# A new order for a clustered attention with a SoLU layer: the first batch's pairs one after another, its first marks copied by three engines

## The chip, the cores and the metric

One core of a Trainium2 chip. The metric is the device time of one execution in microseconds (us). Engines are named as in the profile: PE (TensorE matmul; PEld its weight loads), DVE (VectorE), ACT (ScalarE), POOL (GpSimd), SP (SyncE, which issues nearly all DMAs here).

## The reference

Four batches, eight heads, 768 tokens, 64 channels. Every query and key of a head goes to one of 16 clusters (the largest normalised product with the head's centroids); a query sees the keys of its own cluster only. The 3072 tokens, all heads side by side (512 channels), then pass a layer with 1024 hidden channels.

```python
q_assign = np.argmax(np.einsum('bhsd,hcd->bhsc', q_n, c_n), axis=-1)
k_assign = np.argmax(np.einsum('bhsd,hcd->bhsc', k_n, c_n), axis=-1)
mask = q_assign[:, :, :, None] == k_assign[:, :, None, :]
scores = np.where(mask, scale * np.matmul(q, k.transpose(0, 1, 3, 2)), -1000000000.0)
attn = softmax(scores)                       # over the keys
x = np.matmul(attn, v)  ->  [3072, 512]
...
h = x @ w_in
solu = h * softmax(h)
ln = (solu - mean(solu)) / np.sqrt(var(solu) + 1e-06) * g_ln
return ln @ w_out
```

## The kernel before, in words

**Steps and lists.** All work is recorded as small named steps (a kind and an index), each with an engine. `Weave.ORDER` (lines 28 to 73) is a list for each engine, written by hand as kinds with counts: "S2 V3" means the next two S steps, then the next three V steps. `AWAY` (74 to 90) names the steps that go to another engine than their default. Each engine works through its list in that order. Which S or V is next follows from `UNITS`, `GROUPS` and `BANKS` (256 to 313), the order in which the heads and query blocks are taken.

**Attention.** The unit of heads is a pair (two heads, 128 channels); four pairs a batch, sixteen in all.

- `ld`, `lv` (SP): loads of q, k and of v. Batch 0 is loaded with tokens on the partitions and turned on PE (`tp`, line 382; copied back to SBUF by `xa`, 389), the other batches are turned in blocks of 32 by DVE (`xt`, 404).
- `ca` (423): cast of q or k of one head to bf16 into the tile `qk`; `cv` (531): cast of v.
- `cl` (438, PE): scores of tokens and centroids; `tb`, `mx`, `oh`, `ot` (456 to 494, DVE): turned back, maximum, one-hot marks, turned again; `pl` (498): the marks are copied under the channels of `qk`, four copies a pair (or a half pair), so that one matmul over 80 or 96 rows gives score and mask together; `bl` (521): the other head's marks blanked.
- `S` (594, PE): one bank of scores, 512 columns in most units: two key tiles by 256 queries. Three score banks (`sps`). `E` (604, ACT): the exponential of a bank, 294 in all. Nine tiles (`e`).
- `V` (615, PE): the sum over the values for 128 queries of one head, six matmuls, 192 in all. `N` (628, DVE): normalisation of a group of up to six V into `x`. There is one tile `ops` for the groups' sums, so a group's first V waits for the N of the group before (line 1055).

Pair (0, 0) is done in two halves, so that the first scores can start on half of the tokens. In batch 0 before, the other three pairs were taken by thirds of the queries: `FIRST` (line 280) gives the first and second thirds of pairs 1, 2, 3 in turn, then the last thirds. The other batches take, for pairs 0 to 2, all queries of one head and then all of the other; pair 3 by thirds; the last batch ends by query tiles.

**Second half.** 24 token tiles of 128. `tx` (677, DMA transpose by SP, two tiles at a time; the last by PE, `ptx`): x turned, once all heads of those tokens are normalised. `h` (708, PE): four steps of two matmuls into `hreg`, three banks. `hm` (714, DVE): the maximum; `ex` (719, ACT): the exponential of 1024; `u` (725, DVE): the product; `tu` (730, DMA transpose by SP; last two tiles by PE, `ptu`); `bn`, `ag` (735, 740, DVE): statistics; `at`, `al` (745, 751, POOL): the factor alpha; `y` (760, PE): four steps of two matmuls; `sc` (776, ACT or DVE): scaled by alpha; `ou` (793, SP): stored.

**Weights.** w_in is loaded (`li`) and cast (`wi`); w_out is loaded (`lo`), scaled by g and centred, so that the layer's mean need not be taken off: `gt`, `gk`, `gs` turn and spread g, `su` (570, PE) sums w_out's rows, `sk` (578) copies the sums to SBUF, `me` (583, PE) spreads their mean, `ce` (586, DVE) writes the centred rows. `wm` and `fl` are matmuls on nothing, at the start (line 854).

`run` (124) works out a time for each step from the steps' costs; it sets the order in which steps are recorded, and no step's place in its engine's list.

Of the kernel before, what the change touches and what calls it, by code (L numbers as in the profile page):

```python
# [22 lines left out]
class Weave:  # L23
# [5 lines left out]
    ORDER["SP"] = """
        ld4 lv si ld4 lv lg ld4 lv2 ld4 lo2 ld4 lo ld3 lo ld3 li4 tx ld3 lv3 tx ld4 tu ld9 lv ld tu  # L30
        tx ld3 tu ld3 ou ld2 ou ld tu ld12 tu ld4 lv ld2 ou tx ld3 tu ou ld2 tx lv ld tu ld4 tx ld
        tu ou2 ld lv ld4 tu ld4 tu ld ou ld7 pl ou ld lv2 ld3 tu lv tx ou tu lv pl ld4 ou2 tx lv tu
        tx ou tu pl2 tu2 tx tu tx ou2 tx ou tu tx2 ou tu2 ou2 tu2 ou6
    """
    ORDER["POOL"] = """
        po z ca2 pl2 cv z bl pl2 ca z ca pl2 ca z2 ca3 cv ca cv ca pl3 sg ca cv2 pl3 ca2 gs pl ca cv
        ca wi ca pl2 wi3 bl ca pl2 cv at cv pl ca pl al bl at cv ca pl ca pl cv ca3 al at ca al ca
        at ca pl2 bl cv pl2 ca4 at ca2 al ca pl2 bl pl2 cv2 ca3 al at pl2 bl pl2 ca pl al ca3 at cv
        at pl ca pl2 ca2 pl al cv2 bl cv2 pl2 ca pl al pl at al at pl2 ca3 at al bl cv pl2 bl cv2
        ca3 pl5 al cv3 at al ca2 cv ca cv ca2 at ca2 pl ca al pl2 at2 pl3 at ca cv al at2 al2 at2 al  # L40
        at al3 at al2 at2 al2
    """
    ORDER["PE"] = """
        wm tp2 cp tp cl tp fl5 cl fl4 S3 tp2 S2 tp S cq S tp S2 tp2 S2 V3 S cl S tp2 V3 S gt S tp S
        tp S2 cl S2 V2 S V S2 tp S2 tp S2 V2 S V S2 cl S2 V2 S V2 S3 V S2 V2 S2 V S cl S3 su S2 V3 S
        V S3 V3 S2 V S su S2 V S V3 S3 me S3 V4 S3 cl S3 V4 S2 h S h S2 h S h S2 V3 S2 V h S h V S V
        S h S V S V S h S2 V3 S2 V h S2 h V2 S y3 S2 h3 S3 y V3 h V S2 V2 S cl S3 h2 S2 V3 S y2 S V
        h2 S V y2 S h S V h S2 h S y3 S2 y V3 h S3 cl V2 S V S y S2 y2 S3 V3 S y S2 V3 S2 cl S V S2
        V2 S h S2 V2 S V S h S2 V2 cl V2 S3 y2 S V S2 V y S2 y V2 S3 h2 S V h S h S2 V h S V S V y2
        S h V y2 S2 V S h3 S cl V S2 V2 S h V cl S3 h2 V y V S3 y2 V S h V3 S y S h S2 h2 S3 V2 y h  # L50
        S V S2 y V3 y S3 h3 y S3 V3 S h S V S V cl S V S h S cl V2 S3 y V2 S y S2 y V2 S3 h y V S3 V
        h V2 S3 cl S2 V2 S y3 S2 y S V3 S V S y S2 V S V3 S2 y2 S3 y V2 S2 h V2 S3 h3 S V S2 V y S V
        h2 V2 S y S2 y V y S h2 S3 cl h V S2 V3 S h V2 S3 h2 S y S2 V h S2 V y2 V4 S3 y h S2 h V h V
        S V S y2 S3 V3 h2 S2 h2 S2 y2 S V S h2 S V3 S2 h S h S2 V S y V2 S V y2 S2 h2 S2 h2 V2 S2 V2
        y S2 h V2 h V S2 h S V h S3 V2 h y S V y3 V h3 S2 y3 S2 y h2 V2 h y h y3 h V h V y4 h ptx h
        y4 h2 y3 h2 y ptu2 y6 ptu2 y6
    """
    ORDER["DVE"] = """
        cn cb xa ca tb mx oh ot pl2 tb mx oh ot xa3 bl cf cv xa zo xa2 tb ca mx oh gk N ot tb pl mx
        xa2 oh xa cv N ot tb pl N xt mx xt N oh ot tb pl2 ca N pl xt mx N sk oh N ot xt ce3 N tb ce5  # L60
        N hm mx N u oh ot bn N bn ag hm xt2 u N bn2 hm ag sc xt u N bn tb hm mx bn oh ag u xt bn ot
        xt N cv hm bn ag sc xt tb mx N u xt oh ot sc N bn2 xt ag xt tb N hm mx tb N oh ot u xt mx N
        bn oh bn xt hm ot ag N cv u bn2 xt hm tb mx u N tb oh mx hm ot bn2 oh ag u N sc ag hm bn ot
        u bn N xt2 ag xt2 hm tb N bl mx tb bn2 oh u N xt ag xt sc hm ot tb mx oh N bn sc N u bn N ag
        xt ot bn ca N mx sc oh hm u bn ag N xt hm bn2 bl tb u ot ag N hm mx bn2 u bn N oh ot hm bl2
        u ag N cv hm sc bn u N hm ag bn N bn u bn2 hm ag2 N bn u bn2 N ag hm bn u N ag hm bn2 u bn2
        hm sc u N ag2 bn tx hm bn sc u bn ag hm bn tu ag u bn2 tu ag sc
# [1182 lines left out]
```

## Time and profile before

| | us |
|---|---|
| median of 3 runs | 225.69 (225.38 to 227.81) |
| the profiled execution | 225.95 |
| its span, first to last instruction | 223.9 |

The span is what the profile shows; about 2 us of the execution lie around it. A row of the list of instruction groups reads: line, engine, operation, what it writes and reads, count, then busy time, mean ns of one, and the engine's idle time before it. Some of the costliest:

```
L607 ACT ACTIVATE e<-sps 128x512 bf16<-128x512 f32 (+1 forms) x294 | 151.0, 599 | 12.2 <-PE sps L601 10.2
L727 DVE TENSOR_TENSOR u<-e_sb,hreg 128x1024 bf16<-128x1024 bf16 x24 | 29.0, 1210 | 4.9 <-ACT e_sb L722 4.7
L738 DVE BATCH_NORM_STATS2 bs<-u 128x6 f32<-128x512 bf16 x48 | 31.5, 676 | 0.2
L716 DVE TENSOR_REDUCE nmax<-hreg 128x1 f32<-128x1024 f32 x24 | 29.0, 1209 | 2.6 <-PE hreg L710 2.2
L722 ACT ACTIVATE e_sb<-hreg,nmax 128x1024 bf16<-128x1024 f32 x24 | 26.9, 1120 | 4.5 <-DVE nmax L716 4.4
```

The first score begins at 10.16 us, the first attention exponential at 10.52, the first tile's exponential `ex` at 50.4, the last one at 214.6; the last matmul ends at 220.7.

### The profile page before, as it was taken

To read this page: it belongs to the slowest core of one execution; us is meant where nothing else is said; L and a number is where in the kernel's file an instruction comes from. 1 tells how busy PE (TensorE), PEld (TensorE's weight loads), DVE (VectorE), ACT (ScalarE), POOL (GpSimd) and SP (SyncE) were. 2 spreads that over 40 slices of the span, in tenths; PEclk is the share of its full clock that TensorE was granted. 3 is DMA by queue.
4 is the path that set the end of the run, shared out by engine and by line. 5 is a ranking of instruction groups with operands and counts; after the bars stand their busy time and mean duration, and the time that the engine had idled before them with its cause. 6 is when DMAs were issued, how large, how long until landed. Compare 5 with 4: busy or idle time off the path is not lost.

```text
span 223.9 us, 6574 instructions
## 1 busy us (share of the span) xinstructions
PE 215.1 (96%) x2388; PEld 148.1 (66%) x2420; DVE 197.3 (88%) x359; ACT 191.5 (86%) x371; POOL 127.1 (57%) x247
## 2 busy tenths in 40 slices
PE   7899999999999999999999999999999999999993
PEld 3576756677667678776677667777677687754442
DVE  3799899899999989999998989887998889888981
ACT  3689999999998999998889899999999998982362
POOL 3489843964794999547668634943895413031331
PEclk9999999999999999999999999999999999999999
DMA  7998989999898989999999999199931433766622
GB/s 152 353 318 147 249 199 275 290 243 158 132 199 140 232 130 165 193 189 177 183 218 168 184 195 195 65 174 232 236 64 28 79 70 120 96 146 170 176 97 94
DMA packets 125679, 38.80 MB, mean 173 GB/s; under 512 B 115016, under 2 KB 121168, under 8 KB 125648
## 3 DMA queue, kind: packets, MB, share of 16 engines
q1 hardware_dynamic: 123904, 37.87, 80.6%
q10 hardware_dynamic: 1744, 0.52, 1.0%
q8 instruction: 19, 0.31, 0.6%
q14 instruction: 12, 0.10, 0.2%
HBM read 23.11 MB, written 6.29 MB: 131 GB/s over the span
## 4 chain that ended last, share of the span: by engine, by line
PE 86%; ACT 5%; DVE 3%; issue 3%; DMA 1%; POOL 1%; ACTq 0%; DVEq 0%; POOLq 0%
PE sps L601 28%; PE hreg L710 18%; PE yps L771 16%; PE ops L624 14%; ACT e L607 5%; PE csc L450 4%; PE hreg L386 2%; PE hreg L574 1%; PE hreg L771 1%; DMA c_all<-in_centroids_dram 1%; PE csc L445 1%; DVE bs L738 1%; DVE u L727 1%; ACT xt L393 0%; PE hreg L584 0%
## 5 line engine op out<-in xcount | busy, mean ns | idle before, releaser
L607 ACT ACTIVATE e<-sps 128x512 bf16<-128x512 f32 (+1 forms) x294 | 151.0, 599 | 12.2 <-PE sps L601 10.2
L601 PE MATMUL sps<-qk 80*128 80x256 bf16 (+5 forms) x636 | 93.8, 264 | 1.8 <-POOL qk L514 0.7
L601 PEld LDWEIGHTS <-qk 80*128 80x128 bf16 (+1 forms) x636 | 60.2, 121 | 27.9 <-issue 9.0
L624 PEld LDWEIGHTS <-e 128*128 128x128 bf16 x1152 | 50.4, 97 | 12.3 <-issue 1.9
L624 PE MATMUL ops<-v,e 128*128 128x65 bf16 x1152 | 55.0, 193 | 0.1
L710 PE MATMUL hreg<-w_in_sb,xT 128*128 128x512 bf16 x173 | 49.1, 379 | 1.1
L771 PE MATMUL yps<-w_out_c,uT 128*128 128x512 bf16 x171 | 46.4, 379 | 0.6
L727 DVE TENSOR_TENSOR u<-e_sb,hreg 128x1024 bf16<-128x1024 bf16 x24 | 29.0, 1210 | 4.9 <-ACT e_sb L722 4.7
L514 POOL COPY qk<-oht 32x384 f32<-32x384 f32 (+1 forms) x50 | 24.4, 488 | 15.8 <-DVE oht L494 13.6
L738 DVE BATCH_NORM_STATS2 bs<-u 128x6 f32<-128x512 bf16 x48 | 31.5, 676 | 0.2
L716 DVE TENSOR_REDUCE nmax<-hreg 128x1 f32<-128x1024 f32 x24 | 29.0, 1209 | 2.6 <-PE hreg L710 2.2
L722 ACT ACTIVATE e_sb<-hreg,nmax 128x1024 bf16<-128x1024 f32 x24 | 26.9, 1120 | 4.5 <-DVE nmax L716 4.4
L433 POOL CAST qk<-xt 64x768 bf16<-64x768 f32 (+1 forms) x31 | 26.1, 842 | 5.5 <-DVE xt L393 3.9
L771 PEld LDWEIGHTS <-uT 128*128 128x128 bf16 x200 | 18.2, 97 | 12.3 <-DVE uT L704 0.7
L754 POOL TENSOR_SCALAR esq<-es,mv 128x1 f32<-128x1 f32 x24 | 8.5, 355 | 29.0 <-DVE mv L742 20.8
L435 POOL TENSOR_SCALAR qk<-xt 64x768 bf16<-64x768 f32 (+1 forms) x28 | 23.0, 820 | 1.7
L710 PEld LDWEIGHTS <-xT 128*128 128x128 bf16 x192 | 16.8, 97 | 9.4 <-issue 0.6
L407 DVE STREAM_TRANSPOSE xt<-raw 128x768 f32<-128x768 f32 x24 | 22.6, 953 | 0.2 <-DMA raw<-in_q_dram 0.2
L748 POOL TENSOR_SCALAR es<-esum 128x1 f32<-128x1 f32 x24 | 5.3, 221 | 27.6 <-ACT e_sb L722 27.1
L649 DVE TENSOR_TENSOR x<-ops,den 128x256 bf16<-128x256 f32 (+1 forms) x39 | 18.9, 486 | 1.3
L757 POOL TENSOR_TENSOR alpha<-esq,halves 128x1 f32<-128x1 f32 x24 | 13.5, 561 | 2.0
L786 ACT ACTIVATE y<-yps,alpha 128x512 f32<-128x512 f32 x13 | 9.0, 692 | 6.4 <-PE yps L771 6.0
(80 smaller groups left out, 170.1 us busy)
## 6 DMA issues: line engine op xcount, KB each, us to landing
vf<-in_v_dram SPq DMA_DIRECT2D x16, 384.0 KB, 4.4
out_dram<-y SPq DMA_DIRECT2D x23, 256.0 KB, 2.7
raw<-in_q_dram SPq DMA_DIRECT2D x50, 96.0 KB, 3.7
raw<-in_k_dram SPq DMA_DIRECT2D x50, 96.0 KB, 3.0
w_g<-in_moe_w_out_dram SPq DMA_DIRECT2D x4, 512.0 KB, 5.3
w_st<-in_moe_w_in_dram SPq DMA_DIRECT2D x4, 512.0 KB, 5.9
raw<-in_q_dram SPq DMA_DIRECT2D x3, 384.0 KB, 6.3
raw<-in_k_dram SPq DMA_DIRECT2D x3, 384.0 KB, 6.8
```

Of the source, the lines that this page charges most:

```text
L433: VEC[e].tensor_copy(dst, src)
L435: VEC[e].tensor_scalar(dst, src, scalar1=inv_C, scalar2=1.0, op0=Alu.mult, op1=Alu.mult)
L514: ins = VEC[e].tensor_copy(dst.bitcast(F32), src.bitcast(F32).unsqueeze(1) .to_broadcast([NB, 2, n // 2]))
L601: nc.tensor.matmul(sps_[n, k][:, c0:c0 + w], side(b, h // 2, 1, h % 2, keys)[r], side(b, h // 2, 0, h % 2, slice(s0 * P, s0 * P + w))[r])
L607: nc.scalar.activation(es[n, k][:, :w], sps_[n, k][:, :w], Act.Exp, scale=exp_scale, bias=-exp_scale)
L624: nc.tensor.matmul(opss[g][:, s, :VW], es[n, k][:, c0:c0 + P], v1[slot(b, h // 2)][:, h % 2, kt, :VW], start=(kt == 0), stop=(kt == n_t - 1))
L710: uses(nc.tensor.matmul(hreg[:, at(f, f2)[1], :], xTs[f][:, dc, :], w_in_sb[:, dc, f2 * FF2:(f2 + 1) * FF2], start=(dc == 0), stop=(dc == ...
L716: uses(nc.vector.tensor_reduce(ff[f, "nmax"][:], pair_of(f), axis=AXY, op=Alu.max, negate=True), *both(f))
L722: uses(nc.scalar.activation(ff[f, "e"][:], pair_of(f), Act.Exp, bias=ff[f, "nmax"][:], accum_out=ff[f, "esum"][:]), *both(f))
L727: uses(nc.vector.tensor_tensor(ff[f, "u"][:], ff[f, "e"][:], pair_of(f), op=Alu.mult), *both(f))
L738: nc.vector.bn_stats(ff[f, "bs"][:, f2, :], ff[f, "u"][:, f2, :])
L771: ins = nc.tensor.matmul(dst, ff[f, "uT"][:, at(f, f2)[0] * (n_fc // 2) + c, :], w_out_c[:, fc, cols], start=(fc == 0), stop=(fc == n_fc - 1))
```

## The change

Batch 0 loses its own order: pairs 1 and 2 are now taken as in the other batches, all queries of a head in one go (groups of six V), pair 3 by thirds. The marks of a step in halves may be copied by ACT too. The other edits outside the lists are numbers for `run` (`wm` 3.55 to 3.9, `tp`).

```diff
-    FIRST = [(p, s) for p in range(1, n_pair) for s in range(2)] + [(p, 2) for p in range(1, n_pair)]
     for b in range(B):
...
-            elif b == 0:
-                if p == 1:
-                    for p2, s in FIRST:
-                        GROUPS.append([unit(b, "A", 2 * p2 + j, s) for j in range(2)])
-                        for n in GROUPS[-1]:
-                            in_order(n)
             elif b < B - 1 and p < n_pair - 1 or b == B - 1 and p < n_first:
...
         elif e == "SP":
             ins = nc.sync.dma_start(out=dst, in_=src.unsqueeze(1).to_broadcast([NB, 2, n]))
+        elif e == "ACT":
+            ins = nc.scalar.copy(dst, src.unsqueeze(1).to_broadcast([NB, 2, n]))
...
-                costs = ({"DVE": 0.3, "POOL": 0.41} if half else
+                costs = ({"DVE": 0.3, "POOL": 0.41, "ACT": 0.42} if half else
```

All five lists and `AWAY` are written anew. The ACT list and what goes to ACT and DVE:

```diff
     ORDER["ACT"] = """
-        wa xa2 ca2 xa ca2 E12 xa2 E6 xa E58 ex E12 ex E8 ex E8 ex E3 sc E5 ca E2 ex E25 ex E9 sc E6
-        ex E5 sc E2 ex E9 ex E8 ex E9 sc E6 ex E18 ex E21 ex E5 sc E3 ex E9 ex E7 sc E2 ex E7 ex E8
-        ex E7 ex E6 sc E ex E2 sc E3 ex E2 sc ex sc ex sc ex sc tu2 sc2 oz
+        wa xa2 ca2 xa ca pl ca E3 xa E4 xa E2 pl xa2 E46 sk E32 ex E9 ex E11 ex E7 sc E4 ex E17 ex
+        E12 ex E5 ca E7 ex E sc E6 ex E3 ca E4 sc E2 ex E13 ex E21 ex E11 ex E3 ca sc E5 ex E10 ex
+        E5 sc E6 ex E2 ca E sc E4 ex E5 sc E7 ex E6 sc E2 ex sc E5 ex E sc E3 ex E2 sc E2 ex E2 sc E
+        ex E2 sc ex sc ex sc tu sc2 oz
...
-        ca0.0.0.0.0 ca0.0.0.1.1 ca1.3.1.1 sc23.0 tu22.1 xa0.0.1.0 xa0.2.1.0 xa0.2.1.1 xa0.3.0.0
+        ca0.0.0.0.1 ca0.0.0.1.1 ca2.1.0.1 ca2.2.1.1 ca3.1.1.1 ca3.3.1.0 pl0.0.0.1.0 pl0.0.1.0.1
+        sc23.0 sk xa0.0.0.1 xa0.0.1.0 xa0.1.0.0 xa0.1.1.1 xa0.2.0.1 xa0.2.1.1
     """.split(), "ACT"))
...
-        bl0.0.1 bl2.2 bl3.1 bl3.2 bl3.3 ca0.0.1.0.0 ca0.1.1.0 ca1.0.0.1 ca3.1.1.0 cv0.0.0 cv0.2.0
-        cv1.2.0 cv2.0.0 cv3.3.0 pl0.0.0.1.1 pl0.1.0.0 pl0.2.1.1 pl0.3.0.0 pl0.3.0.1 pl0.3.1.0 sc0
-        sc10 sc13 sc17 sc19 sc2 sc23.1 sc3 sc6 sc8 sc9 tu22.0 zo
+        bl2.2 bl3.0 bl3.1 bl3.2 bl3.3 ca0.0.0.0.0 ca0.0.0.1.0 ca0.0.1.0.0 ca0.1.0.0 ca0.1.0.1
+        ca0.2.0.1 ca0.2.1.1 ca0.3.0.0 ca1.0.0.0 ca1.0.0.1 ca1.1.0.1 ca2.2.0.0 ca3.2.1.1 ca3.3.0.1
+        cv0.1.0 cv0.2.0 cv0.2.1 cv1.0.1 cv1.1.0 cv1.3.0 cv3.0.0 cv3.2.0 cv3.3.0 cv3.3.1 pl0.0.0.1.1
+        pl0.1.1.1 pl0.2.1.1 sc1 sc17 sc19 sc2 sc23.1 sc5 sc6 sc7 tu22.0 wi1 xa0.0.0.0 zo
     """.split(), "DVE"))
```

Steps by engine, where their number changes:

| engine | before | after |
|---|---|---|
| PE | 9 fillers | 8 fillers |
| ACT | 6 `xa`, 5 `ca`, 14 `sc`, 2 `tu` | 7 `xa`, 8 `ca`, 17 `sc`, 1 `tu`, 2 `pl`, 1 `sk` |
| DVE | 39 `N`, 10 `xa`, 4 `ca`, 5 `cv`, 7 `pl`, 11 `sc`, 2 `tu`, 1 `sk` | 37 `N`, 9 `xa`, 14 `ca`, 10 `cv`, 5 `pl`, 8 `sc`, 3 `tu`, 1 `wi` |
| POOL | 59 `ca`, 57 `pl`, 27 `cv`, 4 `wi` | 46 `ca`, 52 `pl`, 22 `cv`, 3 `wi` |
| SP | 4 `pl` | 9 `pl` |

The lists' beginnings, by names (batch.pair.q or k.head, with the half for pair 0.0):

- DVE before: `cn cb xa0.0.0.1 ca0.0.1.0.0 tb0.0.0 mx oh ot pl0.0.0.1.1 pl0.0.0.0.0`; after: `cn xa0.0.0.0 cb ca0.0.0.0.0 ca0.0.0.1.0 ca0.0.1.0.0 tb0.0.0 mx oh ot pl0.0.0.1.1 pl0.0.0.0.0`.
- POOL before: `po z1 ca0.0.0.0.1 ca0.0.0.1.0 pl0.0.0.1.0 pl0.0.0.0.1 cv0.0.1`; after: `po cv0.0.0 cv0.0.1 pl0.0.0.0.1 bl0.0.0`. Later after: `pl0.1.0.0 gs sg cv0.1.1 z1 pl0.1.0.1`, where `gs` follows `gt`, which PE has behind `S4.1`.
- SP after: the first two w_out loads stand inside batch 1's first loads, all four ahead of `lv0.3`; `pl1.0.0.0` stands ahead of `ld1.2.1.2 ld1.2.1 tx0`.
- PE's end, after the last S: before `y h2 V2 h y h y3 h V h V y4 h ptx h y4 h2 y3 h2 y ptu2 y6 ptu2 y6`; after `h y3 h2 y V4 y2 ptx y2 h4 y4 ptu2 y7 ptu2 y5`.

More of the change, by code (lines that the diff above doesn't have):

```diff
@@ L29 @@
     ORDER["SP"] = """
[L30 to L33, printed above, removed]
+        ld4 lv si ld4 lv ld lv ld3 lg ld lo2 ld5 lo2 ld2 lv ld3 li3 ld3 lv ld3 li ld3 pl ld2 tx ld6
+        tx ld lv ld3 lv ld tu tx lv ld2 tu ld7 lv2 ld10 ou tu2 ld6 tx ld3 lv tu ou tx ou lv ld5 ou
@@ L34 @@
+        ld tu ld4 tu tx ld4 ou ld3 lv ou ld5 lv ld3 tu ou ld2 lv ld tu ld tu pl tx ld2 lv ld2 ou pl3
+        tx2 tu3 ou pl3 ou pl tu2 ou tx ou2 tu tx2 tu ou2 tu tx tu ou tx tu ou2 tu ou tu ou5
     """
     ORDER["POOL"] = """
[L36 to L38 removed]
@@ L39 @@
-        at pl ca pl2 ca2 pl al cv2 bl cv2 pl2 ca pl al pl at al at pl2 ca3 at al bl cv pl2 bl cv2
-        ca3 pl5 al cv3 at al ca2 cv ca cv ca2 at ca2 pl ca al pl2 at2 pl3 at ca cv al at2 al2 at2 al
-        at al3 at al2 at2 al2
+        po cv2 pl bl pl2 bl ca5 pl2 gs sg cv z pl3 ca pl cv ca z ca pl2 z ca cv z pl ca2 pl3 wi3 pl
+        ca2 bl ca cv pl2 at bl pl2 ca z ca2 pl cv3 pl3 al at bl pl2 al at bl pl ca cv pl ca2 al ca4
+        pl3 ca pl bl at2 cv3 al ca cv al ca2 at pl3 cv pl bl cv ca at2 ca cv ca pl4 at al ca2 al2
@@ L42 @@
+        ca3 pl2 cv bl pl4 ca3 cv pl at ca al at2 ca3 at ca al ca pl ca cv pl2 cv2 al pl2 at2 al at
+        al2 at al2 at al2 at4 al4 at2 al2
     """
     ORDER["PE"] = """
[L44 to L56, printed above, removed]
+        wm tp2 cp tp cl tp fl5 cl fl3 S3 cq tp S tp S2 tp2 S2 tp S tp S cl V tp2 V2 S2 cl S2 V3 S
+        tp2 S3 tp S2 V S V2 S2 tp S3 gt S V3 S3 cl S2 V S2 V S2 V S V3 S3 su S2 V2 S V S2 V3 S3 cl
@@ new lines @@
+        S2 V S V2 S2 V3 S2 su S3 me S2 V2 S2 V2 S V2 S4 V2 S2 V2 S2 cl S2 V S V2 S V S4 V2 S V2 S2 h
+        S h S h S h V S3 cl V S V S h2 S V3 S2 h2 S3 h2 V S V2 S V3 S cl S3 h2 S2 h V2 S3 y2 V4 S3 y
+        h S y S2 V3 S h2 S2 V2 S V S y2 S3 h y2 S h V S2 V3 S2 V h S V S2 cl S V S2 V h S V S V S h
+        S2 V2 S cl h S V S V3 S2 h S h S2 y V S V3 S y3 S V S2 V y S2 y S h S2 h V2 h S2 h S y S2 y
+        h V5 S3 h V h2 S3 cl h2 S3 V3 y2 S2 V2 y V y S2 h2 S3 h y2 h S2 V y V S2 V3 S h V S y S2 h S
@@ new lines @@
+        V2 S2 y S y3 S V4 h S3 cl S V S2 h V2 S2 V S cl S2 h S V2 h S3 cl V S V S V2 S V S V S y S
+        y2 V h S V S2 V2 y S2 h S h2 S2 V S V3 S2 y2 S2 y2 h V4 S2 h S h2 S2 cl S2 h V h V2 S2 V S
+        cl V h S2 h2 S V S2 y h y S2 V4 S y S2 V y S2 h2 S V S h2 S3 V4 y2 S y S y V S V h S2 h y S
+        y2 S V S h2 y S V S2 h2 V3 S2 h V S h S2 V3 S V S2 y S V S y V y2 S2 V2 S h2 S V S2 y h2 S
+        y3 V S V2 h2 y S V S y2 h2 y S2 V2 S h2 V S2 y3 S2 y h V2 h3 S y V2 y3 S h S2 h3 y3 S y h S
@@ L57 @@
+        h y3 h2 y V4 y2 ptx y2 h4 y4 ptu2 y7 ptu2 y5
     """
     ORDER["DVE"] = """
[L59 to L67, printed above, removed]
+        cn xa cb ca3 tb mx oh ot pl2 tb mx oh ot cf xa2 ca2 pl xa tb xa zo mx oh ot cv ca N xa pl tb
+        xa mx xa2 gk oh N cv tb ot cv ca2 N xt pl xt mx oh ca ot N ca xt tb N mx oh ot ce2 ca xt N
@@ new lines @@
+        ce wi N ce3 xt N tb ce mx xt N oh ce cv hm xt ot u tb N bn hm mx cv xt u N tb bn oh hm ot mx
+        oh ag N bn u bn ag ot xt hm bn xt bn cv N u bn sc ag bn N xt2 tb hm mx N oh u tb N ot ag hm
+        bn N mx sc oh u bn2 xt ag N hm xt ot u bn N ca hm tb xt bn mx u bn oh bn2 hm ot ag N u xt2 N
+        sc bl hm ag2 xt2 sc N u tb mx xt oh ot bn cv tb mx bn N oh tb bn hm N ot mx oh u bn N xt sc
+        hm bn xt ag N ot u ag xt bl N hm xt bn tb u bn tb mx2 hm N bn oh2 u ag ot bl hm N bn cv ot u
@@ L853 @@
                             scalar1=c_inv[:], scalar2=None, op0=Alu.mult)
-    add("wm", "PE", 3.55, -1000, lambda e: [idle(FF2) for _ in range(6)])
+    add("wm", "PE", 3.9, -1000, lambda e: [idle(FF2) for _ in range(6)])
     for j in range(sum(int(x or 1) for x in re.findall(r"\bfl(\d*)", wv.ORDER.get("PE", "")))):
@@ L905 @@
                 n2 = [f"ld{t}.{hf}" if halves_of(b, p) else f"ld{t}"] + ring_h[-3:-2]
-                add(f"tp{t}.{hf}", "PE", 0.7 - 0.2 * hf if halves_of(b, p) else 0.36, first - 15 + i + hf,
+                add(f"tp{t}.{hf}", "PE", (0.5 if i * hf else 0.7) if halves_of(b, p) else 0.36, first - 15 + i + hf,
                     (lambda e, b=b, p=p, i=i, hf=hf: turn_tokens(b, p, i, hf)), n2,
```

13 lines of the change are left out of this document (7 added, 6 removed).

## The prediction, made before the run

> **What bounds the kernel now.** I read the page's busy shares first, then PE's chain of waits, then the windows, then the rows of the copies that the change moves.
>
> ```profile
> span 223.9 us, 6574 instructions
> PE 215.1 (96%) x2388; PEld 148.1 (66%) x2420; DVE 197.3 (88%) x359; ACT 191.5 (86%) x371; POOL 127.1 (57%) x247
> PE 86%; ACT 5%; DVE 3%; issue 3%; DMA 1%; POOL 1%; ACTq 0%; DVEq 0%; POOLq 0%
> ```
>
> The chain that ended last is 86% PE, but three engines are above 85% busy, and a busy PE row also holds waiting. So I price PE's work by its unbroken pieces in the chain of waits (start, us, what):
>
> ```profile
> 43.58 0.78 PE csc L450 x8
> ...
> 45.89 0.44 PE sps L601 x4
> ...
> 48.50 0.43 PE hreg L710 x2
> ...
> 49.38 0.57 PE ops L624 x18
> ...
> 203.00 1.29 PE yps L771 x6
> ```
>
> A bank of scores (S, two matmuls) is 0.22 us, a sum over the values (V, six) 0.19, a quarter of a token tile's h or y 0.43, a pair's cluster scores 0.78. All of it: S 63.0, V 36.5, h 41.5, y 41.5, cluster scores 13.3, token transposes 6.6, w_out's sums, the turns and small ones 4.6: 207.0 us. PE works from 4.13 to 220.7, 216.5 us, so only 9.5 us are lost. Where:
>
> ```profile
> core 0: us, PE busy (x) PEld busy (x) DVE busy (x) ACT busy (x) POOL busy (x), PEclk, DMA share, GB/s
> 20.00:25.00 5.00, 4.71 (x66) 3.40 (x66) 4.67 (x11) 4.89 (x12) 4.62 (x10) 1.00 0.74 214
> 25.00:30.00 5.00, 4.89 (x77) 3.46 (x70) 4.34 (x8) 4.84 (x11) 4.00 (x8) 1.00 0.82 163
> 50.00:55.00 5.00, 4.61 (x55) 3.56 (x54) 4.55 (x11) 4.97 (x11) 1.60 (x4) 1.00 0.89 150
> 100.00:110.00 10.00, 9.89 (x110) 6.15 (x111) 9.49 (x16) 8.98 (x18) 6.21 (x11) 1.00 0.91 169
> 215.00:220.00 5.00, 4.50 (x33) 2.46 (x31) 3.55 (x8) 3.26 (x7) 1.99 (x5) 1.00 0.28 105
> ```
>
> Before the first token tile reaches the second half (to about 55 us) ACT is nearly full with exponentials, and PE, which has 0.22 + 0.13 us of work for each 0.5 us of ACT's, waits: in 20 to 45 us its pieces add up to 22.0 of 25 us. From 55 to 200 us they add up to 142.5 of 145: there PE is the bound, with DVE at about 92%. The rest is lost before the first score (10.16 us; 3.5 us of work done since 4.13, so 2.5 lost) and about 1.1 in the last chain.
>
> **The change, part by part.** No matmul but one filler is added or taken (0.14 us, granted clock 1.00 in every window; cost nothing). PE's 207.0 us stay, so the time moves only by what PE loses.
>
> *First marks.* The first score waits for POOL's two mark copies (9.35 to 10.11). Now POOL has one, DVE still two (9.25 to 9.83), ACT one. ACT's list ahead of it: two copies (0.48) and three casts (0.52) from 5.7 us on, with waits for transposes, to about 9.4; the mark has no row on ACT, nearest are the cast of 384 columns, 0.52, and the copy, 0.48: it ends at 9.8 to 9.9. DVE now does a copy and three casts (0.34 each) before the first turned cluster scores; they fit before 7.5, where those arrive anyway. First score at about 9.95; the first exponential stands behind one more ACT cast, at 10.35 instead of 10.52. Gain 0.2; none if the copy on ACT takes 0.3 longer.
>
> *Natural order.* Batch 0's first token tiles need all heads. Before, three pairs' first thirds sufficed; now pairs 1 and 2 are done whole first. In ACT's list the first tile's exponential stands behind 87 instead of 76 attention exponentials. Adding up PE's list: ahead of the 89th bank 47.3 us of work before, 45.6 after. ACT reaches that bank at about 58 us in both (before: 57.3 plus one tile exponential of 1.1; after: one tile exponential less by then, against one copy, w_out's sums and two marks more, 0.5 each). So PE has 1.7 us less done at the same time. Against it: pair 2 starts at bank 43 instead of 37, pair 3 at 61 instead of 49, so their casts and marks can't be late; attention exponentials took 0.57 us each at 31 to 42 us, 0.49 at 21 to 31, and PE waited 0.6 to 0.8 us at a time for POOL's marks. Between 0 and +1.7; I take +1.2, since ACT's pace there was mostly its own.
>
> *The middle.* The debt grows to 5.9 us of PE work by bank 200 (122.9 against 117.0), is gone by bank 285, and after the last bank 15.5 us remain instead of 19.9. So the h and y work lies denser late. Whether DVE can follow: its list changes by 8 full casts and 2 half ones (+4.9 to +6.6), 5 v casts (+2.1), a w_in cast (+0.7, by width from the cast below), one uT copy (+0.4), minus three y scalings (2.2), sums' copy (0.7), a token copy (0.5), marks (1.1), two normalisations (0.6): +3 to +5 on 197.3. ACT: three scalings, three casts, sums, marks, a copy, less a uT copy: +6 on 191.5. POOL: about 17 less, off the path. DVE's rows, start to next start: h maximum and u 1.13 each, statistics 0.60, transposes 0.89, normalisation 0.64 or 0.52. Between the normalisations after the 96th and the 108th V, DVE has 14.7 us of work to PE's 12.2 (before: 14.1 to 13.6); over the whole list, cut every 12 sums from the 48th on, DVE exceeds PE by 5.1 us in sum where it exceeds it (before 1.5). A late normalisation stops the next V, as there is one ops tile; nine tiles of exponentials and three score banks ride over part. Between 0 and +3.6; I take +0.7, nearer to nothing because over 36 sums at a time (84 to 120: PE 36.6, DVE 34.7) PE stays longer.
>
> *Ports.* The moved copies:
>
> ```profile
> L433 POOL CAST qk<-xt 64x768 bf16<-64x768 f32 x29 | 25.0, 864 | 1.5
> L532 DVE CAST v<-vf 128x384 bf16<-128x384 f32 x5 | 2.1, 426 | 0.0
> L433 DVE CAST qk<-xt 64x768 bf16<-64x768 f32 x1 | 0.7, 742 | 0.0
> ...
> 32.74 1.26 DVE L506 COPY qk<-w_out_c 16x384 f32<-16x384 f32 x2
> ```
>
> Two mark copies of one shape: 0.35 us the first, 0.88 the second, which begins at 33.12 while a POOL cast runs from 32.96 to 33.79. Other DVE copies show 0.1 to 0.24 over their shortest; 17 of them lose 1.1 us, 0.07 each. Fourteen more: 0.9 us on DVE, inside its slack in the opening, where most stand. The Trainium skill (SBUF — State Buffer, section Who interferes with whom) states that DVE's two-port copies and GpSimd take one shared port pair, exclusively for a whole instruction; the 0.88 agrees. By the row the sum stays as it is below; by the rule alone each moved copy can be held for a whole POOL cast, and the sum would be rival (b)'s.
>
> *Queues.* On SP the first w_out loads go ahead of batch 1's, the last v load of batch 0 behind all four of them (landing at about 30 us by the pace before, needed past 40), nine mark DMAs instead of four (2.2 us to land); one stands ahead of three loads and the first x turn, and waits for DVE; the turn waits longer anyway. On POOL the spreading of g stands earlier and waits for a PE transpose behind unit 4's second bank; behind it lie a v cast and a mark of head 3, 1.7 us of work, due nine banks (4.3 us) later. w_out's sums copied on ACT: 0.58 beside three banks in hand. All nothing; if one cover fails, 1 to 2 us in the opening.
>
> *End.* From the last h to the last y: 7.6 us before with 6.5 of PE work in it; the list now puts 7.8 us of work there (four y quarters of tile 20 and all of 21 and most of 22), so the chain maximum, exponential, u, turn is covered but for about 0.4. Gain 0.7.
>
> Sum: -0.2 + 1.2 + 0.7 - 0.7 = +1.0. The profiled execution took 225.95 (span 223.9 and 2.05 around it), 0.26 over the median 225.69. So 226.95 beside it, **226.7** as a median: within 1%, which is about what can be told from no change.
>
> **Rivals.** (a) DVE becomes the bound in the middle: the 3.6 us stand in full and 0.9 of held copies in front of normalisations: +1.0 - 0.7 + 4.5 = +4.8, 230.5. For: the stage sums; DVE was 92% busy there. Against: over longer stretches PE's work is more. It decides once PE's waits for normalisations exceed those before by 2 us. (b) Held copies: the second mark copy of 33.12 us is the rule and not the exception, fourteen moved copies are held by 0.2 to 0.5 each (seen: 0.07 on average, 0.53 at most) with half of it on the path: +1.0 + 3.0 = +4.0, 229.7. Against: POOL has 17 us less, so meetings are rarer. The Trainium skill's page on SBUF speaks for it. (c) Faster: with pairs 2 and 3 due later the opening runs at 0.49 us a bank (-1.7), PE's waits for marks go (-0.6), half of the 2 us that PE loses from 58 to 200 goes with POOL's relief (-1.0), and the end: -0.2 + 1.2 - 1.7 - 0.6 - 1.0 - 0.7 = -3.0, 222.7. For: POOL's copies were late there. Against: ACT and DVE carry more. (d) The marks on ACT don't bring the first score forward: 226.9.
>
> **Chances.** Forecast 0.39, (d) 0.03, (a) 0.27, (b) 0.08, (c) 0.23. Faster by over 1% 0.23, within 0.42, slower 0.35. The range reaches into (c) and to (a)'s end, 222.6 to 230.6; the forecast's own is 224.3 to 228.
>
> **What would show it.** First score before 10.0; tile 0's exponential at 55.5 to 57.5 us with about 7 us lost by PE; bank 200 reached 2 to 5 us earlier than the 135 before; the last S 4 us before the old distance from the end. Wrong, if PE's idle behind normalisations grows by more than 2 us (a), DVE's casts have means above 0.9 us (b), or the 87 exponentials are through before 54 us (c).

## The result, and the profile after

The changed kernel takes 228.77 us (median of 6 runs, 228.30 to 229.54); the kernel before, run beside it, 225.74 (6 runs). The ratio is 1.0125, with a 95% interval of 1.0095 to 1.0154: 3.0 us slower. The profiled execution took 228.57, its span is 226.5 (before 225.95 and 223.9). Forecast were 226.7 and a range of 222.6 to 230.6: the time lies in the range, 2 us above the forecast. The range is 8 us wide and holds two rivals' times as well; the forecast's own, 224.3 to 228, was missed.

The page of the changed kernel, span, engines and the chain that ended last:

```profile
span 226.5 us, 6598 instructions
PE 218.8 (97%) x2419; PEld 146.9 (65%) x2419; DVE 201.3 (89%) x365; ACT 196.2 (87%) x380; POOL 112.7 (50%) x223
PE 84%; DVE 5%; ACT 4%; issue 3%; DMA 2%; SPq 1%; ACTq 0%; DVEq 0%
```

DVE has 4.0 us more than before (forecast 3 to 5), ACT 4.7 more (6), POOL 14.4 less (17). PE's share of the chain fell by two points and DVE's rose by two. Line numbers are 5 to 7 lower than before (S is L596, V L619, h L705).

The same windows as in the prediction, of the changed kernel:

```profile
core 0: us, PE busy (x) PEld busy (x) DVE busy (x) ACT busy (x) POOL busy (x), PEclk, DMA share, GB/s
20.00:25.00 5.00, 4.90 (x63) 3.22 (x65) 4.89 (x12) 5.00 (x13) 1.06 (x4) 1.00 1.03 214
25.00:30.00 5.00, 4.69 (x68) 3.08 (x60) 4.55 (x10) 4.89 (x11) 3.45 (x7) 1.00 1.13 278
50.00:55.00 5.00, 4.78 (x52) 3.42 (x51) 4.82 (x11) 4.94 (x11) 1.61 (x3) 1.00 0.99 163
100.00:110.00 10.00, 10.00 (x110) 6.62 (x108) 9.41 (x15) 9.78 (x20) 8.57 (x17) 1.00 0.94 208
215.00:220.00 5.00, 5.00 (x36) 2.67 (x35) 4.00 (x8) 2.47 (x4) 2.20 (x6) 1.00 0.31 108
```

In the opening ACT is as full as before, and PE's busy share says little, since it counts waiting between matmuls. So the prediction's ledger is kept up: the time at which a bank's first weight load begins, less 4.13 (where PE begins in the kernel before; the same is taken off for both), less the pieces that stand ahead of it in PE's list. What is left is PE's loss up to that bank. Banks are counted from 0.

| PE reaches | before: at us / lost | after: at us / lost | growth of the difference |
|---|---|---|---|
| first bank | 9.9 / 2.3 | 9.7 / 2.1 | -0.2 |
| bank 24 | 22.2 / 2.3 | 22.3 / 2.3 | +0.2 |
| bank 48 | 34.4 / 3.5 | 35.2 / 4.3 | +0.8 |
| bank 89 | 57.0 / 5.4 | 57.3 / 7.2 | +1.0 |
| bank 200 | 134.3 / 7.0 | 130.7 / 8.9 | +0.1 |
| bank 293, the last | 199.5 / 8.2 | 206.1 / 10.5 | +0.4 |
| last step of y | 220.0 / 9.3 | 222.4 / 11.7 | +0.1 |

The opening lost most: 1.8 of 2.4. Bank 89 comes at nearly the same time in both kernels, with 1.5 us less of PE's work done ahead of it (47.5 before, 46.0 after, by the same ledger).

The table is one execution of each kernel and no more. Traces of the experiments below that share these kernels' opening tell what repeats (us; banks and y by their first weight load, the first score by its matmul):

| | first score begins | from there to bank 24 | bank 24 to 89 | bank 89 to 293 | bank 293 to the last y |
|---|---|---|---|---|---|
| kernel before | 10.16 | 12.0 | 34.9 | 142.5 | 20.5 |
| before, its end moved | 9.85 | 12.0 | 34.9 | 142.5 | 20.5 |
| before, one cast moved | 9.78 | 12.0 | 35.2 | 142.5 | 20.5 |
| changed kernel | 9.77 | 12.6 | 35.0 | 148.8 | 16.3 |
| changed, first marks back on POOL | 10.01 | 12.6 | 34.9 | 148.8 | 16.3 |
| changed, held casts back on POOL | 10.53 | 12.5 | 34.8 | 148.7 | 16.3 |
| changed, the middle's casts on POOL | 10.23 | 12.5 | 34.9 | 148.7 | 16.3 |
| the same, and the end reordered | 10.09 | 12.6 | 34.9 | 148.7 | 15.6 |
| changed, end reordered | 10.14 | 12.5 | 34.9 | 148.8 | 15.6 |

From the first score to the last y it is 209.8 us in the kernel before (209.8 and 210.1 in its relatives) and 212.6 in the changed kernel (212.4 to 212.6 in the three with its end): 2.8 more. What differs most between executions is when the first score begins, and the profiled pair lies at the far ends of that: the -0.2 of the first table's first row (0.4 by the matmul) is not shown to be the change's doing.

Where DVE took over the chain of waits in the opening (start, us, what; changed kernel):

```profile
29.18 0.21 DVE den L631
...
29.89 0.97 DVE xt L400
...
31.27 0.98 DVE xt L400
32.25 0.45 DVE mx L465
32.70 0.02 issue
32.72 0.60 DVE w_out_c L471
33.32 1.10 DVE qk L426
34.42 0.88 DVE w_out_c L484
35.30 0.09 DVE den L631
```

From one normalisation (29.18) to the next (35.30; the expectations below call it the third) there is nothing but DVE, among it two turns of raw blocks, a maximum, the one-hot marks (0.60), one moved cast of q or k (1.10) and the marks' turn. In the trace before there is no such stretch in the opening. The cast is long beside one of POOL's. POOL's time line, then DVE's:

```profile
32.88 1.13 POOL L428 TENSOR_SCALAR qk<-xt 64x768 bf16<-64x768 f32 x1
...
34.56 0.83 POOL L428 TENSOR_SCALAR qk<-xt 64x768 bf16<-64x768 f32 x1
```

```profile
32.72 0.60 DVE L471 TENSOR_TENSOR w_out_c<-cst,mx 128x384 bf16<-128x384 f32 x1
33.25 1.18 DVE L426 CAST qk<-xt 64x768 bf16<-64x768 f32 x1
...
36.01 0.56 DVE L426 CAST qk<-xt 64x768 bf16<-64x768 f32 x1
```

The next of each take 0.83 and 0.56 us; side by side they took 1.13 and 1.18. POOL's ends at 34.01, DVE's cast 0.42 later, as if most of its work had waited until there. The Trainium skill (SBUF — State Buffer, section Who interferes with whom) gives this as an exclusive hold for one whole instruction, and the trace agrees.

### The profile page after: what moved, and what is told of

It is laid out like the page before. It is cut to its first block, busy times and chain, and to the rows that moved or that the text cites. A ratio compares the mean times of both kernels' runs of the same rounds, so it can differ in the third digit from the quotient of the medians.

```text
span 226.5 us, 6598 instructions
## 1 busy us (share of the span) xinstructions
PE 218.8 (97%) x2419; PEld 146.9 (65%) x2419; DVE 201.3 (89%) x365; ACT 196.2 (87%) x380; POOL 112.7 (50%) x223
## 4 chain that ended last, share of the span: by engine, by line
PE 84%; DVE 5%; ACT 4%; issue 3%; DMA 2%; SPq 1%; ACTq 0%; DVEq 0%
PE sps L596 27%; PE hreg L705 18%; PE yps L766 16%; PE ops L619 15%; PE csc L443 4%; ACT e L602 3%; PE hreg L379 2%; DMA raw<-in_q_dram 2%; PE csc L438 1%; ACT y L781 1%; DVE xt L400 1%; PE hreg L766 1%; DVE bs L733 1%; DVE u L722 1%; ACT e_sb L717 0%
## 5 line engine op out<-in xcount | busy, mean ns | idle before, releaser
L596 PE MATMUL sps<-qk 80*128 80x256 bf16 (+5 forms) x636 | 96.6, 264 | 1.4 <-DVE qk L509 0.2
L596 PEld LDWEIGHTS <-qk 80*128 80x128 bf16 (+1 forms) x636 | 60.1, 121 | 28.6 <-issue 10.9
L619 PEld LDWEIGHTS <-e 128*128 128x128 bf16 x1152 | 49.9, 97 | 11.2 <-issue 2.1
L619 PE MATMUL ops<-v,e 128*128 128x65 bf16 x1152 | 54.4, 193 | 0.3 <-DVE x L644 0.3
L705 PE MATMUL hreg<-w_in_sb,xT 128*128 128x512 bf16 x192 | 52.9, 379 | 0.0
L766 PE MATMUL yps<-w_out_c,uT 128*128 128x512 bf16 x184 | 48.7, 378 | 0.1
L509 POOL COPY qk<-oht 32x384 f32<-32x384 f32 (+1 forms) x42 | 21.0, 500 | 37.7 <-DVE oht L487 31.9
L705 PEld LDWEIGHTS <-xT 128*128 128x128 bf16 x192 | 17.1, 97 | 11.6 <-DVE u L722 1.2
L400 DVE STREAM_TRANSPOSE xt<-raw 128x768 f32<-128x768 f32 x24 | 22.7, 957 | 0.1
L428 POOL TENSOR_SCALAR qk<-xt 64x768 bf16<-64x768 f32 (+1 forms) x26 | 21.6, 829 | 2.5 <-ACT xt L386 0.8
L644 DVE TENSOR_TENSOR x<-ops,den 128x384 bf16<-128x384 f32 (+1 forms) x37 | 18.6, 503 | 1.3
L781 ACT ACTIVATE y<-yps,alpha 128x512 f32<-128x512 f32 x16 | 11.1, 693 | 8.9 <-PE yps L766 7.2
L426 POOL CAST qk<-xt 64x768 bf16<-64x768 f32 x20 | 16.9, 844 | 1.0
L527 POOL CAST v<-vf 128x384 bf16<-128x384 f32 x22 | 11.3, 529 | 6.5 <-DMA vf<-in_v_dram 6.2
```

The costliest lines, as they stand in the source:

```text
L400: nc.vector.transpose(xt[:], raws[b, p, i][:].rearrange("p j c -> p (j c)"))
L428: VEC[e].tensor_scalar(dst, src, scalar1=inv_C, scalar2=1.0, op0=Alu.mult, op1=Alu.mult)
L596: nc.tensor.matmul(sps_[n, k][:, c0:c0 + w], side(b, h // 2, 1, h % 2, keys)[r], side(b, h // 2, 0, h % 2, slice(s0 * P, s0 * P + w))[r])
L619: nc.tensor.matmul(opss[g][:, s, :VW], es[n, k][:, c0:c0 + P], v1[slot(b, h // 2)][:, h % 2, kt, :VW], start=(kt == 0), stop=(kt == n_t - 1))
L705: uses(nc.tensor.matmul(hreg[:, at(f, f2)[1], :], xTs[f][:, dc, :], w_in_sb[:, dc, f2 * FF2:(f2 + 1) * FF2], start=(dc == 0), stop=(dc == ...
L766: ins = nc.tensor.matmul(dst, ff[f, "uT"][:, at(f, f2)[0] * (n_fc // 2) + c, :], w_out_c[:, fc, cols], start=(fc == 0), stop=(fc == n_fc - 1))
```

## The experiments

Each was run beside the kernel before, whose medians were 225.53 to 226.19 in the four sets; times are medians.

**Is PE's time in the opening free?** Eight banks, every fourth from 44 to 72, are computed twice, the second time over the first, which adds 8 x 0.22 = 1.75 us to PE and to nobody else:

```diff
-        for h, kt, s0, w, c0 in u["banks"][k]:
+        for h, kt, s0, w, c0 in u["banks"][k] * (1 + (BANKS.index((n, k)) in range(44, 76, 4))):
```

> The changed kernel with eight banks of scores computed twice (every fourth of banks 44 to 72, in the opening; the same matmuls into the same bank, 0.22 us each, 1.75 us of PE work more; the output stays). Theory A (the opening runs at ACT's pace, and PE only lacks h work there): PE's time is free here, so the 89th bank and the end stay where they are, within 0.4 us of the changed kernel (228.8). Rival (PE waits for late marks, casts or normalisations in the opening, each on the chain): the work adds up, +1.2 to +1.8 us, about 230.3.

229.09 (ratio 1.0166, 1.0137 to 1.0196): 0.3 over the changed kernel, within theory A's 0.4, so by the medians most of the 1.75 was free. The trace says otherwise: bank 89 comes at 58.6 instead of 57.3, so 1.3 of the 1.75 came through, and PE's loss fell only from 7.2 to 6.7, though the changed kernel lost 1.8 us between banks 48 and 72. But the profiled execution took 229.80, 0.7 over its median, while four of the six took 229.25 or less. The medians speak for theory A; how much of PE's time is free there, wherever the work is put, stays open between 0.4 and 1.4 of the 1.75 us.

**Who bounds the middle?** The same with the banks 200, 204, ... 228.

> The same with every fourth of banks 200 to 228 in the middle. Theory A (from the 90th bank on PE is the bound): the whole 1.75 us come through, 230.2 to 230.7. Rival (DVE bounds the middle of the changed kernel): less than 0.7 us comes through, below 229.5.

231.30 (1.0238, 1.0212 to 1.0264). By the ledger, with the doubled banks counted as work, the loss grows by 0.8 us between banks 200 and 240, and by 1.0 without them: the 1.75 came through but for 0.2. The median lies above the 230.2 to 230.7 expected; the trace has 0.8 of that by bank 24 already, its first score having begun at 10.52. PE bounds the middle; rival (a) is not what happens.

**The first marks back on POOL.** `pl0.0.0.1.0` and `pl0.0.1.0.1` leave ACT's list and stand in POOL's, the one ahead of `bl0.0.0`, the other behind the first of the casts that follow.

> The changed kernel with the two first marks that ACT copies back on POOL, as before. Theory A (the gain at the first score is gone by bank 24, and ACT's pace sets the opening from there): the first score goes from 9.74 to about 10.0 us, the end moves by less than 0.4 us. Rival (the marks on ACT are worth what the first score gains): +0.2 to +0.5 us.

228.87 (1.0146, 1.0119 to 1.0172), the changed kernel's time. Its first bank comes 0.1 later and its last y 0.2, less than executions of one kernel differ by. In POOL's list both marks still stand behind two v casts, which the kernel before has after its marks.

**The end in another order.** On DVE the last maximum ahead of the second half of tile 22's statistics, on ACT the last exponential ahead of `sc20`, `sc19` from DVE to ACT, the last copy of u ahead of the second half of the last statistics:

```diff
  DVE
-  ... tx u sc bn2 ag2 hm tu2 u bn2 tu ag sc
+  ... tx u bn hm ag bn ag tu2 u bn tu bn ag sc
  ACT
-  E ex E2 sc ex sc ex sc tu sc2 oz
+  E ex E2 sc ex sc ex sc2 tu sc2 oz
  PE
-  ... ptx y2 h4 y4 ptu2 y7 ptu2 y5
+  ... ptx y2 h4 y4 ptu2 y5 ptu2 y7
```

> The changed kernel with another order of the last steps: on DVE the last maximum (hm23) ahead of the statistics of tile 22, the scaling of tile 19 on ACT instead of DVE, on ACT the last exponential ahead of the scaling of tile 20, the last u turn on PE two y steps earlier and its copy ahead of the second half of tile 23's statistics. Theory T (the gain that I gave the end, 0.7 us, was eaten by DVE's list ahead of hm23, 0.9 us, and by ACT's scaling, 0.35 us): 0.4 to 0.9 us faster than the changed kernel, 227.9 to 228.4. Rival (the end is bound by PE's work alone): within 0.2 us.

227.96 (1.0102, 1.0085 to 1.0118), 0.8 under the changed kernel. DVE's time line at the end, first of the changed kernel:

```profile
213.38 0.74 DVE L783 TENSOR_SCALAR y<-yps,alpha 128x512 f32<-128x512 f32 x1
214.04 1.27 DVE L733 BATCH_NORM_STATS2 bs<-u 128x6 f32<-128x512 bf16 x2
215.23 0.33 DVE L737 BATCH_NORM_AGGREGATE mv<-bs 128x2 f32<-128x12 f32 x2
215.47 1.17 DVE L711 TENSOR_REDUCE nmax<-hreg 128x1 f32<-128x1024 f32 x1
```

of this one:

```profile
213.73 0.69 DVE L734 BATCH_NORM_STATS2 bs<-u 128x6 f32<-128x512 bf16 x1
214.82 1.23 DVE L712 TENSOR_REDUCE nmax<-hreg 128x1 f32<-128x1024 f32 x1 [0.40 <-PE hreg L706]
```

and of the kernel before:

```profile
213.34 1.22 DVE L716 TENSOR_REDUCE nmax<-hreg 128x1 f32<-128x1024 f32 x1 [0.39 <-PE hreg L710]
```

In the changed kernel the last h was done at about 214.55, and the maximum begins 0.9 later with no idle time ahead of it: a scaling, two statistics and two sums of tiles 21 and 22 stand ahead of it in DVE's list. Here it waits for PE (0.40), as it did in the kernel before (0.39). On ACT a scaling stood ahead of the last exponential, which begins 0.4 after the maximum ended (216.64); changed kernel:

```profile
216.45 0.69 ACT L781 ACTIVATE y<-yps,alpha 128x512 f32<-128x512 f32 x1 [4.67 <-PE yps L766]
217.04 1.11 ACT L717 ACTIVATE e_sb<-hreg,nmax 128x1024 bf16<-128x1024 f32 x1
```

From the last bank to the last y it took 15.6 us here, 16.3 in the changed kernel.

**The held casts.** `ca1.0.0.0` and `ca1.0.0.1` go back from DVE to POOL, ahead of `pl1.0.1.0`:

```diff
  POOL
-  z pl ca2 pl3 wi3 pl ca2 bl
+  z pl ca2 pl ca2 pl2 wi3 pl ca2 bl
  DVE
-  ca2 N xt pl xt mx oh ca ot N ca xt tb N
+  ca2 N xt pl xt mx oh ot N xt tb N
```

> The changed kernel with the two casts ca1.0.0.0 and ca1.0.0.1 given back from DVE to POOL, just ahead of pl1.0.1.0. Theory D (DVE is what the chain of waits runs on from 29 to 36 us, and the cast that took 1.18 us there beside POOL's own cast stands ahead of the third normalisation): that normalisation ends about 1.2 us earlier, the 48th bank starts 0.4 to 1.0 us earlier than its 35.2, and the time is 0.4 to 1.0 us under the changed kernel: 227.8 to 228.4 beside 228.8 (2.0 to 2.6 over the kernel before). Rival (POOL's sequence is as late with the casts in it, or PE lacks h work there whatever DVE does): within 0.3 of the changed kernel.

228.78 (1.0128, 1.0102 to 1.0155): no gain. This execution began 0.8 later (first score at 10.53). Against that start the normalisation came 0.7 earlier (35.33 beside 35.24), yet bank 48 came 0.7 later (35.9 beside 35.2): 25.4 us after the first score in both. The chain of waits of this kernel, over the same stretch:

```profile
30.80 1.00 PE hreg L570 x8
...
34.14 0.64 ACT e L603
34.78 0.04 issue
34.82 0.38 PE sps L597 x2
35.20 0.78 PE csc L444 x8
```

PE's sums of w_out, ACT's exponentials and the cluster scores stand there now. The stretch on DVE was real, and worth nothing by itself.

**The same cast in the kernel before**, moved from POOL to DVE just ahead of `ot0.3`.

> The kernel before with the one cast ca1.0.0.0 moved from POOL to DVE, just ahead of ot0.3. Theory D: the cast takes 0.7 us there, up to 1.2 beside a cast of POOL's, the chain of normalisations behind it comes that much later, and the time rises by 0.4 to 1.0 us over the kernel before (225.9 to 226.5 beside 225.5). Rival (DVE has slack in the opening of the kernel before, as the prediction has it): within 0.3.

225.82 (1.0002, 0.9977 to 1.0027). The cast took 0.55 us here, beside no cast of POOL's, and the time stayed. So a cast that isn't held costs nothing in DVE's list there; what a held one would cost in the kernel before was not tried. In the changed kernel, where it was held, theory D fell by the experiment before this.

**Turn x and take h earlier.** `tx0` is issued ahead of the mark `pl1.0.0.0` and the loads behind that, and the four steps of `h0` stand two banks earlier on PE (the expectation says about three).

> The changed kernel with tx0 issued ahead of pl1.0.0.0 on SP (it should land about 1.2 us before its 51.85) and the four steps of h0 about three banks earlier in PE's order. If what PE lacks in the opening is h work (the term of 1.2 in the sum), tile 0's exponential comes about 1 us before its 56.75 and the time falls by 0.2 to 0.5 us: 228.3 to 228.6 beside 228.8. If the opening is held by ACT's and DVE's banks alone, 0 or slower by up to 0.3, since PE then waits for tx0 with scores behind it.

229.41 (1.0168, 1.0139 to 1.0197), 0.6 slower than the changed kernel. The turn is issued at 47.59 instead of 48.39 and the first h begins at 52.1 instead of 52.5, but bank 89 comes 1.0 later (58.3) with 1.0 more lost, of which 0.2 was there at the first bank and 0.5 at bank 60, ahead of what was moved. From bank 24 to bank 89 it takes 35.8 us, and 35.9 in the next kernel, which has the same steps moved; the others with the changed order take 34.8 to 35.2 (doubled banks in the opening aside). So the moved steps cost time; by which wait the trace doesn't tell; the sign is against what the expectation made of the prediction's term.

**All three repairs.**

> The changed kernel with three repairs at once: the two casts back on POOL, tx0 and h0 earlier, and the end reordered (hm23 ahead of the sums of tile 22, sc19 on ACT, ex23 ahead of sc20, tu23.1 after bn23.0). If the parts add (about 0.7, 0.3 and 0.8): 226.7 to 227.3, that is 1.2 to 1.8 over the kernel before, which leaves the middle's 0.6 and some of the opening. If the opening's loss is not the casts' or h0's: about 228.0, what the reordered end gave alone.

229.39 (1.0158, 1.0135 to 1.0182). It begins late like the one with the casts back (first bank at 10.5), and carries the loss of the kernel with h earlier (9.0 at bank 89); between the last bank and the last y it takes 15.6 us instead of 16.3, which is the reordered end. Three repairs, of which one was worth something.

**Only the lateness, in the kernel before.** Nothing is changed but the place of tiles 0 to 4 in every list. PE's part around bank 72:

```diff
-  S2 h S h S2 h S h S2 V3 S2 V h S h V S V
-  S h S V S V S h S2 V3 S2 V h S2 h V2 S y3
+  S8 V3 S2 V S V S V h S2 h V S V h S2 h S
+  V3 S2 V S h S h V2 S h S2 h S3 V2 h V2 h
```

> The kernel before with nothing changed but the place of the second stage's work on tiles 0 to 4: every step of it (h, the maxima, exponentials, u, the sums, y, scaling, the transfers of u and of the output) that began between 46 and 57 us is put 6.4 us later in its engine's order, those from 57 to 88 us later by less and less, down to nothing. So tile 0's first h comes at about 52.5, as in the changed kernel, and about five steps of h (2.2 us of PE) leave the time before the 89th bank; scores, values, clusters and the first stage's work on DVE, ACT and POOL are as they were. Theory H (ACT's exponentials with DVE's chain behind them set when the 89th bank comes, and PE idles for what it lacks): the 89th bank stays at 56.5 to 57.2 in place of 57.0, the loss there rises from 5.4 to about 7, and the time by 1.2 to 2.0 us, to 226.9 to 227.6. Rival (PE sets the opening): the 89th bank comes about 2 us earlier, at 55, the loss stays near 5.4, and the time is within 0.4 of the kernel before.

239.28 (1.0599), far outside both theories; but up to bank 89 it is the test that was wanted. The fairest partner is the next experiment's kernel, identical up to there and with the same start (first bank at 9.7 and 9.6):

| | first bank | bank 89: at us / lost | last y: at us / lost |
|---|---|---|---|
| order before up to here | 9.6 / 2.0 | 56.7 / 5.0 | 219.7 / 9.0 |
| tiles 0 to 4 later | 9.7 / 2.1 | 56.5 / 6.6 | 233.4 / 22.7 |

The bank comes when it came, with 1.7 us of PE's work, four steps of h, gone from ahead of it (the expectation had five), and the loss is 1.6 higher. Busy time from 46 to 57 us, first the partner, then this kernel:

```profile
46.00:57.00 11.00, 10.50 (x128) 8.24 (x129) 10.33 (x19) 10.98 (x24) 6.22 (x13) 1.00 1.05 223
```

```profile
46.00:57.00 11.00, 9.93 (x121) 7.51 (x123) 7.28 (x15) 10.26 (x20) 4.16 (x8) 1.00 1.13 189
```

The third figure is DVE: 3 us of it are free now, so DVE doesn't hold the banks back. ACT, the fourth, waited 0.7 us between 44 and 57 us, 0.2 in the partner, and its exponentials otherwise run end to end (waiting, waited for: us, times, longest; the partner first):

```profile
ACT e L607 <- PE sps L601: 0.2, 1, 0.2
```

```profile
ACT e L607 <- PE sps L601: 0.7, 3, 0.2
```

So ACT sets when the bank comes, and PE can't use the time: theory H, for the opening. If the 0.5 that ACT waited more is the shift's own doing, the price is 1.1; else 1.6.

Two cluster scores also stand a few places earlier on PE, behind that bank. There the lists jam, and the total is no measure of theory H: each engine's list was moved by times from the trace and not by what waits for what. PE at the worst place:

```profile
63.89 0.85 PE L450 MATMUL csc<-xt,c_bd 128*32 128x384 f32 x8
67.33 1.01 PE L771 MATMUL yps<-w_out_c,uT 128*128 128x512 bf16 x2 [2.58 <-DVE cst L459]
```

**The end of the kernel before** in the manner of the repaired end: the four steps of `y17` behind `h21.1.1`, the turn of the last x behind `h22.1.1`, the copy of the last u ahead of half of the last statistics.

> The kernel before with three steps of its end moved: the four steps of y17 behind h21.1.1, the transposition of x's tile 23 behind h22.1.1, and the copy of the last u ahead of the second half of the sums of tile 23. If the end is a chain of h, maximum, exponential and u from tile to tile, as the repair of the changed kernel's end showed, the chain starts y17's time earlier and the time falls by 0.3 to 0.9 us, to 224.8 to 225.3; if PE has no idle time left there to move, within 0.2.

225.77 (1.0011, 0.9995 to 1.0028): nothing. The last maximum of the kernel before was not late: it waited for PE.

**DVE's density in the middle.** The ten casts that DVE does after 50 us go to POOL.

> The changed kernel with the ten casts that DVE does after 50 us (seven of v at 0.31 to 0.39 us, three of q or k at 0.56 to 0.63, 4.2 us in all in the changed kernel's trace) given to POOL, each where its time puts it in POOL's list; POOL was busy for half of the span. The prediction's term for the middle (+0.7, DVE's density): if that is what the 0.5 us lost between the 89th and the last bank are, that loss goes from 3.3 back to about 2.8 and the time falls by 0.3 to 0.7 us, to 228.1 to 228.5. If it is not DVE's casts, the loss stays at 3.3 and the time within 0.3 of 228.8.

```profile
PE 219.0 (97%) x2419; PEld 147.2 (65%) x2419; DVE 198.2 (87%) x355; ACT 196.1 (86%) x380; POOL 118.2 (52%) x233
```

228.94 (1.0116, 1.0074 to 1.0157). DVE has 3.1 us less than in the changed kernel and POOL 5.5 more, and from bank 89 to the last it takes 148.7 us instead of 148.8. DVE's casts are not what the middle lost. Together with the reordered end:

> The same with the reordered end, which alone came to 227.96: if both repairs hold and add, 227.3 to 227.7, still about 1.6 to 2.0 over the kernel before, which is the opening's price; if the casts do nothing, about 228.0.

227.95 (1.0084, 1.0056 to 1.0112): 1.0 below the former in the same set, the end's worth for a second time, and none for the casts. No version beat the kernel before; the best order found for the changed one is the one with its end repaired, at 227.96 and 227.95.

## Why the prediction was right or wrong, step by step

- **First marks, -0.2.** The first score begins at 9.77 instead of 10.16, the first exponential at 10.13 instead of 10.52: 0.4, twice the forecast, but by the luck of two executions. The other traces with the old beginning have the first score at 9.78, 9.79 and 9.85, those with the new one between 9.78 and 10.64 (10.01 with the marks back on POOL, and the same time). No gain is shown. What failed is "now POOL has one": the step counted POOL's mark copies and not what stands ahead of them. POOL's new list begins with two v casts, which wait for v's load; in the kernel before they come after the marks. In the kernel with banks of the middle doubled the load landed late, POOL's mark came last, and the first score began at 10.52:

```profile
8.99 0.96 POOL L527 CAST v<-vf 128x384 bf16<-128x384 f32 x2 [5.45 <-DMA vf<-in_v_dram]
10.01 0.46 POOL L509 COPY qk<-oht 32x192 f32<-32x192 f32 x1
```

- **Natural order, +1.2 of 0 to 1.7.** The mechanism is the one named: tile 0's exponential begins at 56.75 (50.36 before; forecast 55.5 to 57.5) with 7.2 us lost (forecast about 7), the exponential of bank 89 begins at 58.8 (58.9 before), and the work missing ahead of the bank is 1.5 (forecast 1.7). Lateness alone, in the kernel before, cost 1.1 to 1.6 there. From the first score to bank 89 the loss grew by 2.2 more than before, past the upper bound: 1.5 for the work and 0.7 for coming 0.7 later against the first score. Of the 0.7, 0.6 are ahead of bank 24, where PE has 0.2 us more work; what the rest waits for stays open. The failed step is the deduction for late casts and marks, 0.5 taken off because the banks might come sooner: from bank 24 to 89 they took 35 us as before, and nothing was given back. Between the first exponential and 57 us ACT waited for scores 1.2 us, 1.1 before, so late marks did not set the pace.
- **The ports, 0 beside it.** That the held copies lie "inside its slack in the opening" was wrong of DVE, which was the chain from 29 to 36 us, and right of the time: taking the two casts away gained nothing, adding one that wasn't held in the kernel before cost nothing. Rival (b) asked for casts of 0.9 us on the mean; DVE's nine took 692 ns:

```profile
L426 DVE CAST qk<-xt 64x768 bf16<-64x768 f32 x9 | 6.2, 692 | 0.1
```

- **The queues, 0.** "The turn waits longer anyway" was wrong: the last normalisation for tile 0 ended at 47.12 and the turn was issued at 48.39, behind the mark's DMA and two loads. But issuing it earlier, with h0 earlier, did not make the kernel faster.
- **The middle, +0.7.** By the ledger +0.5 (from bank 89 to the last). The size was hit and the reason was not: DVE's casts, the term's largest part, can go without effect. PE's waits for normalisations (its matmuls' and its weight loads' together) grew from 0.8 us to 2.1 over the whole span, 1.3 more, under the 2 that rival (a) asked for. Of them 0.6 lie behind bank 89, in one wait for DVE that is as long with the casts on POOL. The row of the sums over the values, with its idle time last:

```profile
L619 PE MATMUL ops<-v,e 128*128 128x65 bf16 x1152 | 54.4, 193 | 0.3 <-DVE x L644 0.3
```

  Where the 0.5 come from stays open; they lie somewhere in the 200 banks behind bank 89. The debt went as forecast: bank 200 at 130.7 (forecast 2 to 5 before 135), 16.3 us from the last bank to the last y instead of 20.5.
- **The end, -0.7.** It came to +0.1, and reordering three lists brought 0.8. The step counted the work that PE has beside the chain of maximum, exponential and u, and took the chain's links to start when their inputs are there. It didn't look at what DVE and ACT had ahead of those links: 0.9 us on DVE ahead of the last maximum, 0.4 on ACT ahead of the last exponential.

Forecast were +1.0 and measured 3.0 as medians. Of the 2.0 between them 0.2 are the first marks, which gave nothing, 1.0 is the natural order (2.2 for 1.2) and 0.8 the end; the middle gives 0.2 back, and 0.2 lie behind the start of the last y. So the loss is the one that was named, work made late in the opening, in a size that the range of its term did not reach. That the total still lies in the range is no merit of the sum: the range was drawn to hold rivals (a) and (c). The likeliest case, within 1%, did not come by the median, 1.25% (the interval begins at 0.95%); slower by over 1% had 0.35, but by rivals (a) and (b), and neither is what happened.

## What to carry to other kernels

Work that a reordering makes late costs what the bounding engine can't do meanwhile: add up that engine's list ahead of a point which another engine paces, before and after, and take the difference in full, as here, unless a trace shows that the pacing engine will come sooner. In a chain across engines each link has its own list: for the last links, read what stands ahead of each on its own engine. A stretch of the chain of waits on one engine is not yet a price: taking it away can put another engine there. And where the start varies, compare two traces from their first score on, not from the start of the span.
